# A gated mix of memory attention and a GLU: narrower memory update, new planner lengths and a seeded order of the fillers

## The chip, the core and the metric

The kernel runs on one core of a Trainium2 chip. The metric is the device time of one execution in microseconds; lower is better. An unprofiled run gives only that time. One more execution is recorded by the hardware profiler, and the profile and trace that are shown here come from it.

The engines are called as the profile calls them: PE is TensorE (its weight loads are PEld), DVE is VectorE, ACT is ScalarE, POOL is GpSimd, SP the engine that issues most of the DMAs.

## What is computed

`x` is 2048 x 512, bf16. Two branches work on it and a gate mixes them:

```python
g = sigmoid((x * gate_w).sum(-1))
out = g * attention(x) + (1 - g) * glu(x)

# glu: 512 -> 1792 -> 512
h = gelu(x @ w_gate) * (x @ w_up);  b = h @ w_down

# attention: 32 heads of 16, four segments of 512 rows, one after the other
for s in range(4):
    p = softmax(qs @ ks.T * 0.25 + causal_mask)
    a_dot = p @ vs
    a_mem = (phi(qs) @ M) / (phi(qs) @ z + 1e-6)     # phi(t) = t+1 if t > 0 else exp(t)
    o = sigmoid(beta) * a_mem + (1 - sigmoid(beta)) * a_dot
    M += phi(ks).T @ vs;  z += phi(ks).sum(rows)     # per head: 16 x 16 and 16
a = o @ wo
```

For each head M is a 16 x 16 block and z a vector of 16. Stored for eight heads on 128 partitions, M is a block-diagonal matrix.

## The kernel before

**Opening.** Weights and x are loaded over the SP queue, with transposing DMAs for the segments 1 to 3 of x. Then the gate half of the GLU runs for all segments at once: 28 `gate_pair` groups, each of eight 128x128 matmuls with 512 columns (L457), one gelu on ACT (L625) for each pair. Among them lies one tiny matmul, `f_bps` (L644), which spreads beta over the partitions; ACT takes its tanh (L673), and DVE derives `omg`, `ebr`, `bdeb` (block-diagonal mask times a factor) and the scaled `wo` from it. In the kernel before, this group stands after the seventh gate pair.

**Main part.** Each segment has 20 logit slots (`logit_slot`, L713). A slot's matmuls use row tiles: 16 or 32 rows, four heads at once. Each slot fills four PSUM banks (two pairs), ACT takes two exps of 128 x 1024 (L735), POOL zeroes what the causal mask hides (L744). Five slots give one chunk of eight heads; `pv_group` (L763) multiplies by v, DVE transposes the result, takes the reciprocal of its sum column and scales (L781 to L807). `N` (L799) and `r` times gate (L794) are operations with both inputs in SBUF.

Between two slots TensorE does fillers, the dense work: `up_group` (the other half of the GLU), `qk_group` and `v_group` for the next segment, `m_update`, `mem_den`, `mem_num`, and `out_group` (w_down and wo for the segment before). Dense products are split into four column tiles of 32 (L461), so that four matmuls run side by side. Each output of a filler is taken from PSUM by DVE or ACT.

**Memory.** `phi` makes an exp on ACT (L825), a maximum and a minimum on DVE (L829, L832), and an addition on POOL (L836). phi(k) is transposed by a DMA into `pk`. `m_update` multiplies it by v, with 8 heads x 17 columns (v and a one) at once: for each of two chunks and four row blocks, four column tiles of 32 weights by 136 columns, of which each tile needs only those of its own two heads. DVE adds the result to `Macc` (L882, L884); after the second pair, one operation makes `Mbd` (L891) and one `zbd` (L894), both with the diagonal masked.

**Order.** A planner in the kernel's file (`Sched`) sets the order of every engine's instructions before they are emitted. Each `add` gives a task its engine, an assumed length in ns, its dependencies, its PSUM banks and its priority. The planner runs a list schedule over these: on each engine the ready task with the lowest priority value goes first; logit slots have a due time, which spreads the remaining dense work over the remaining slots; rings of buffers and the eight PSUM banks hold tasks back. `NUPS` says how many up groups belong to each segment. The order is fixed in the program; each engine then runs its list in that order and waits where an input is late.

Of the kernel before, what the change touches and what calls it, by code (L numbers as in the profile page):

```python
# [1 line left out]

# [9 lines left out]
F32 = dt.float32  # L12

P = 128
D = 512
H = 32
DH = 16
VW = DH + 1
NSEG = 4
L = 512  # L20
KT = L // P
DFF = 1792
FC = D // P
NCH = H // 8
HS = DFF // P
# [9 lines left out]
NWARM = 7  # L35
NUPS = (28, 10, 9, 9)
SHAPES = {"gen": [(b,) for b in range(NBANK)],
# [16 lines left out]
class Sched:  # L54
# [7 lines left out]
    def __init__(self, rings):  # L62
        self.tasks = []
        self.bufs = rings

    def add(self, engs, cost, fn, **kw):

        engs = {engs: cost} if isinstance(engs, str) else dict(zip(engs, cost))
        t = Task(engs, fn, **kw)
        t.seq = len(self.tasks)  # L70
        self.tasks.append(t)
        return t
# [199 lines left out]
def kernel(  # L272
# [38 lines left out]
    def ctile(name, shape, dtype=BF):  # L311
        return cp.tile(shape, dtype, name=name, tag=name)
# [37 lines left out]
    Mbd = ctile("Mbd", [P, NCH, 8, DH])  # L350
    Macc = ctile("Macc", [P, NCH, 8, VW], F32)
    G2 = ctile("G2", [P, NSEG, QB], F32)
# [39 lines left out]
    def ext(at):  # L392
# [26 lines left out]
                            compare_op=ALU.is_ge, fill=0.0, base=DH - 1, channel_multiplier=-1)  # L419
    nc.gpsimd.memset(vz[1][:, :, :], 1.0)  # L420

    def group(name, cost, mms, prio, deps, alloc="gen", also=None, **kw):
# [11 lines left out]

    EV = {"DVE": 610, "ACT": 560}

# [31 lines left out]
    def odd_copy(s, c, ev):  # L468
        pr = c // 2
        ko = ("o", s, pr)  # L470

        def fo(e):
            if ko not in QK:
                QK[ko] = rtile("kO", [P, 2, L])
            nc.vector.tensor_scalar_mul(QK[ko][:, c % 2, :], QK[("k", s, pr)][:, c % 2, :],
                                        odd[:, :])
        new = ko not in first_ev
        o = add("DVE", 400, fo, prio=2, deps=[ev] + ([] if new else [first_ev[ko]]),
                alloc=["kO"] if new else [])
        first_ev.setdefault(ko, o)  # L480
        EVQK[("o", s, c)] = o
# [136 lines left out]
    def gate_pair(s, hp, prio):  # L618
        def mms(t):
            for i in range(2):  # L620
                mm_x(t[:, i, :], wga, (2 * hp + i) * P, s)
        g, box = group("gt", 8 * MM, mms, prio, [a_x[s], a_wg0 if hp < 2 else a_wga], alloc="pair")
        read_x[s].append(g)
        dst = G[:, s, 2 * hp:2 * hp + 2, :]
        ge = evac("ACT", g, box, lambda e, t: nc.scalar.activation(dst, t[:, :, :],  # L625
                                                                  AF.Gelu_apprx_tanh),
                  cost=960, ring="pair")
        GM[(s, hp)] = ge
        TAB["last_gt"], TAB["last_ge"] = g, ge
# [36 lines left out]
    for s in range(NSEG):  # L666
        if s == 3:
            gate_rows(-960 + 20 * s)
        for hp in range(HS // 2):
            gate_pair(s, hp, -959 + 20 * s + hp)  # L670
            if s == 0 and hp == HS // 2 - 1:
                g, box = group("bps", 60, f_bps, -942, [a_be])
                t_tb = evac("ACT", g, box, lambda e, t: nc.scalar.activation(  # L673
                    tb[:, :], t[:, 0:NCH], AF.Tanh, scale=0.5), cost=250)
                t_om = add("DVE", 100, f_omg, deps=[t_tb], prio=5)
                t_eb = add("DVE", 1200, f_eb, deps=[t_om], prio=5)
                t_wo = add("DVE", 1300, f_wo, deps=[t_om, a_wo], prio=7)
# [16 lines left out]
    def logit_slot(s, t):  # L694
# [37 lines left out]
        for h in range(2):  # L732
# [16 lines left out]
            XT_[(gi, h)] = x  # L749
            AT[(gi, h)] = add("POOL", 380 if w in (0, 3) else 610, fa, prio=0, deps=[x])  # L750

    def pv_group(s, c, e):
# [27 lines left out]
        def f_T(_, t):  # L780
            nc.vector.transpose(TT[key][:, e, :, :].rearrange("p a b -> p (a b)"), t[:, :])  # L781
        ev = evac("DVE", g, box, f_T)
        if e == 0:
# [22 lines left out]
        def f_o(_):  # L806
            nc.vector.transpose(xT[:, c, s * L:(s + 1) * L],  # L807
                                NN[key][:, :, :, :].rearrange("p a e d -> p (a e d)"))
        r = add("DVE", 280, f_r, prio=3, deps=[ev, NMT[("Te", key)]], alloc=["r"])
        rg = add("DVE", 120, f_rg, prio=3, deps=[r, TAB["g2"]])  # L810
        n = add("DVE", 650, f_n, prio=3, deps=[rg], alloc=["N"], frees=[("r", r), ("T", T0)])
        last = n
        if s > 0:
            last = add("DVE", 500, f_m, prio=3, deps=[n, NMT[("Nm", key)]],
                       frees=[("Nm", NMT[("Nm", key)])])
        OTT[key] = add("DVE", 640, f_o, prio=3, deps=[last] + read_x[s], frees=[("N", n)])

    PQ, PKt, PHI, PKD, RMt = {}, {}, {}, {}, {}

    def phi(src, deps, prio, mk, ring):  # L820
        box = {}

        def f_e(_):
            box["E"] = rtile("E", [P, 2, L])
            nc.scalar.activation(box["E"][:, :, :], src()[:, :, :], AF.Exp)  # L825

        def f_q(_):
            box["Q"] = rtile("Q1", [P, 2, L])
            nc.vector.tensor_scalar_max(box["Q"][:, :, :], src()[:, :, :], 0.0)  # L829

        def f_m(_):
            nc.vector.tensor_scalar_min(box["E"][:, :, :], box["E"][:, :, :], 1.0)  # L832

        def f_a(_):
            d = mk()
            nc.gpsimd.tensor_add(d[:, :, :], box["E"][:, :, :], box["Q"][:, :, :])  # L836
        e = add("ACT", 980, f_e, prio=prio, deps=deps + [TAB["first_x"], opened], alloc=["E"])
        q = add("DVE", 380, f_q, prio=5, deps=[e], alloc=["Q1"])
        m = add("DVE", 380, f_m, prio=5, deps=[e])
        return add("POOL", 2250, f_a, prio=5, deps=[m, q], alloc=[ring],  # L840
                   frees=[("E", e), ("Q1", q)])
# [23 lines left out]

    def m_update(s, pr, prio):
        def mms(t):
            for i in range(2):
                c = 2 * pr + i
                for kt in range(KT):  # L870
                    dense(t[:, i * 8 * VW:(i + 1) * 8 * VW], PKt[(s, pr)][:, i, kt, :],
                          vz[s % 2][:, kt, 8 * c * VW:8 * (c + 1) * VW], kt == 0, kt == KT - 1)
        g, box = group("M", 8 * 60, mms, prio,
                       [PKD[(s, pr)]] + [EVV[(s, kt)] for kt in range(KT)]
# [4 lines left out]
        def f_acc(e, t):  # L879
            dst = Macc[:, 2 * pr:2 * pr + 2, :, :].rearrange("p c h w -> p (c h w)")  # L880
            if s == 0:
                nc.vector.tensor_copy(dst, t[:, 0:16 * VW])  # L882
            else:
                nc.vector.tensor_add(dst, t[:, 0:16 * VW], dst)  # L884
        acc = evac("DVE", g, box, f_acc, cost=360)
        TAB[("acc", s, pr)] = acc
# [3 lines left out]
        def f_mbd(_):  # L890
            nc.vector.tensor_mul(Mbd[:, :, :, :], Macc[:, :, :, 0:DH], bdeb[:, :, :, :])  # L891

        def f_zbd(_):
            nc.vector.tensor_mul(  # L894
                zbd[:, :].rearrange("p (c n) -> p c n", c=NCH)[:, :, 0:P]
                .rearrange("p c (j m) -> p c j m", j=4)[:, :, :, 0:2],
                Macc[:, :, :, DH].rearrange("p c (j e) -> p c j e", j=4),
                bd[:, :, 0].rearrange("p (j e) -> p j e", j=4)[:, None, :, :]
                .to_broadcast((P, NCH, 4, 2)))
        deps = [TAB[("acc", s, 0)], acc, t_eb] + [TAB[("num", s, c)] for c in range(NCH) if s]  # L900
        TAB[("mbd", s)] = add("DVE", 620, f_mbd, prio=3, deps=deps)
        TAB[("zbd", s)] = add("DVE", 150, f_zbd, prio=3, deps=deps + ([TAB[("den", s)]] if s else []))

    def mem_den(s, prio):
# [25 lines left out]
        ev = evac("DVE", g, box, f_T)  # L930
        a = add("DVE", 200, f_a, prio=2, deps=[ev], alloc=["rm"], frees=[("Tm", g)])
        r = add("DVE", 880, f_r, prio=2, deps=[a])
        TAB[("rm", s)] = add("DVE", 250, f_g, prio=2, deps=[r])
        TAB[("rma", s)] = a

    def mem_num(s, c, prio):
# [13 lines left out]
        def f_n(_):  # L950
# [4 lines left out]
        ev = evac("DVE", g, box, f_T)  # L955
        NMT[("Nm", (s, c))] = add("DVE", 680, f_n, prio=2.5, deps=[ev, TAB[("rm", s)]],
                                  alloc=["Nm"], frees=[("Tm", g), ("rm", TAB[("rma", s)])])
# [15 lines left out]
    def out_group(s, qt, prio):  # L973
# [5 lines left out]
        for lo in range(0, HS, 2):  # L979
            def fn(_, lo=lo):  # L980
                down(bank(first), s, qt, lo, lo + 2, False)
            prev = add("PE", 2 * MM, fn, prio=prio, mode="more" if lo else "open",
                       deps=[prev] if lo else [UPT[(s, hs)] for hs in range(HS)] + [TAB["wdn"]]
                       + ([] if late else att), alloc=[] if lo else ["gen"], final=late)
            first = first or prev
# [4 lines left out]
        def fo(e):  # L990
# [4 lines left out]
            else:  # L995
                nc.vector.tensor_scalar_mul(bx["o"][:, :], bank(first), f)  # L996
        ev = add(["DVE", "ACT"], [670, 590], fo, deps=[g, TAB["omz"]], alloc=["osb"],
                 frees=[("gen", first)])
# [80 lines left out]
```

## Time and profile before

| | before |
|---|---|
| median of 3 runs | 282.32 us (282.3 to 283.6) |
| profiled execution, own time | 284.42 us |
| its span, first to last instruction | 282.7 us |
| busy: PE / DVE / ACT / POOL | 272.1 / 173.2 / 211.3 / 129.1 us |
| opening (0 to 67.1 us), PE busy | 64.6 us |
| logit slots (67.1 to 268 us), PE busy | 196.7 us |
| end (268 to 282.7 us), PE busy | 10.7 us |
| mean granted TensorE clock | 0.994 |

How to read it: a matmul's record is longer than the time until the next one starts, because matmuls are pipelined, so busy PE is not PE at its peak, and a hole between starts is larger than the idle time shown. Lines of the kernel are given as L and a number; L457 and L461 are in the helper `dense`, so most matmuls have one of these two, and the names of tiles tell them apart. In timelines a row has start, length, engine, line, what it writes and reads, shape, count, and in brackets the engine's idle time before it and what ended it. The row of the clock gives tenths of the full TensorE clock in forty slices of the span.

### The profile page before, as it was taken

Reading aid. Unit: us, or ns where it says so; the run is one execution under the profiler, and the core shown is the slowest. Engines: PE = TensorE matmul, PEld = TensorE weight load, DVE = VectorE, ACT = ScalarE, POOL = GpSimd, SP = SyncE. Lnnn points to the kernel's source line nnn. Section 1 sums busy time; section 2 is a strip of 40 time slices with the busy share of each in tenths; the row PEclk is TensorE's granted clock in tenths of the full one; section 3 lists DMA queues with packets and bytes.
Section 4 is the critical chain, followed back from the end, with each engine's and each line's share of the span. In section 5 each row is a group of like instructions: output and inputs, shape, how many; then the busy total and the mean of one; then the engine's idle time right before and its main releaser. Section 6 shows DMA issues by size and latency. Waiting matters only on the chain.

```text
span 282.7 us, 10149 instructions
## 1 busy us (share of the span) xinstructions
PE 272.1 (96%) x4498; PEld 126.6 (45%) x4504; DVE 173.2 (61%) x316; ACT 211.3 (75%) x231; POOL 129.1 (46%) x220
## 2 busy tenths in 40 slices
PE   8999899999999989999999999999999998999994
PEld 3444344444445444454445445444444443444541
DVE  2330210102879898989897797999758699535330
ACT  3545466457897777999898898898889889798520
POOL 8000000060565376486857477457645756444400
PEclk9999999999999999999999999999999998999999
DMA  7963970000022010020010020000000000000011
GB/s 237 345 125 77 339 252 2 0 0 2 3 42 39 2 39 2 2 42 2 21 39 22 3 58 23 3 2 2 21 21 22 2 21 3 21 21 21 23 38 39
DMA packets 22036, 14.02 MB, mean 50 GB/s; under 512 B 14056, under 2 KB 20968, under 8 KB 21992
## 3 DMA queue, kind: packets, MB, share of 16 engines
q1 hardware_dynamic: 21448, 12.85, 16.0%
q8 instruction: 35, 0.57, 0.9%
q10 hardware_dynamic: 544, 0.52, 0.6%
q14 instruction: 9, 0.07, 0.1%
HBM read 8.13 MB, written 2.10 MB: 36 GB/s over the span
## 4 chain that ended last, share of the span: by engine, by line
PE 74%; DVE 8%; SPq 7%; ACT 4%; DMA 2%; issue 2%; POOL 0%; ACTq 0%; DVEq 0%
PE ps L461 48%; PE ps L457 13%; PE ps L713 8%; SPq L360 7%; PE ps L763 5%; ACT pT L735 3%; DMA wdn<-in_A_x_dram 1%; DVE N L799 1%; DVE G L635 1%; DVE vz_82 L299 1%; DMA beta_76<-in_A_beta_dram 1%; DVE r L794 1%; DVE T L781 1%; DVE Nm L952 1%; DVE N L804 1%
## 5 line engine op out<-in xcount | busy, mean ns | idle before, releaser
L735 ACT ACTIVATE pT<-ps 128x1024 bf16<-128x1024 f32 x160 | 153.9, 1025 | 20.9 <-PE ps L713 20.2
L744 POOL TENSOR_SCALAR_AFFINE_SELECT pT<-pT 128x512 bf16<-128x512 bf16 (+1 forms) x160 | 92.5, 586 | 83.1 <-ACT pT L735 82.6
L461 PE MATMUL ps<-wdn,G 128*32 128x512 bf16 x896 | 59.3, 386 | 0.5 <-ACT pT L735 0.5
L461 PE MATMUL ps<-xT,wup 128*32 128x512 bf16 x896 | 55.2, 380 | 0.9 <-DVE G L635 0.8
L635 DVE TENSOR_TENSOR G<-ps,G 128x512 bf16<-128x512 f32 x56 | 37.6, 678 | 20.7 <-PE ps L461 20.3
L457 PE MATMUL ps<-xT,wga 128*128 128x512 bf16 x219 | 48.4, 379 | 0.4 <-issue 0.2
L625 ACT ACTIVATE G<-ps 128x1024 bf16<-128x1024 f32 x28 | 28.7, 1025 | 24.2 <-PE ps L457 23.5
L457 PEld LDWEIGHTS <-wga 128*128 128x128 bf16 x224 | 21.8, 98 | 26.4 <-issue 0.4
L461 PEld LDWEIGHTS <-wup 128*32 128x32 bf16 x896 | 22.3, 96 | 22.9 <-issue 4.7
L461 PEld LDWEIGHTS <-G 128*32 128x32 bf16 x896 | 21.9, 97 | 21.3 <-issue 3.9
L781 DVE STREAM_TRANSPOSE T<-ps 128x512 f32<-128x512 f32 x32 | 22.7, 708 | 13.6 <-PE ps L763 13.4
L596 POOL COPY G_87<-tt 32x16 f32<-32x16 f32 x16 | 3.1, 195 | 49.3 <-DVE tt L588 48.6
L713 PE MATMUL ps<-qT,kT 16*128 16x256 bf16 (+2 forms) x320 | 17.9, 273 | 1.5 <-DVE vz_82 L299 1.2
L713 PE MATMUL ps<-qT,kO 32*128 32x128 bf16 (+2 forms) x320 | 18.5, 276 | 0.1
L461 PEld LDWEIGHTS <-xT 128*32 128x32 bf16 x448 | 11.4, 96 | 11.3 <-issue 1.6
L461 PE MATMUL ps<-wo,xT 128*32 128x512 bf16 x256 | 16.5, 379 | 0.0
L713 PEld LDWEIGHTS <-kT 16*128 16x128 bf16 x320 | 6.9, 92 | 19.4 <-issue 19.1
L799 DVE TENSOR_TENSOR N<-T,r 128x512 bf16<-128x512 f32 x16 | 14.2, 887 | 0.4
L713 PEld LDWEIGHTS <-kO 32*128 32x128 bf16 x320 | 7.1, 93 | 14.8 <-issue 14.6
L994 ACT ACTIVATE osb<-ps,omz 128x512 bf16<-128x512 f32 x6 | 4.1, 687 | 11.5 <-PE ps L461 11.5
L996 DVE TENSOR_SCALAR osb<-ps,omz 128x512 bf16<-128x512 f32 x10 | 7.4, 743 | 8.6 <-PE ps L461 8.5
L461 PE MATMUL ps<-xT,wk 128*32 128x512 bf16 x192 | 12.5, 380 | 0.0
(116 smaller groups left out, 282.1 us busy)
## 6 DMA issues: line engine op xcount, KB each, us to landing
out_dram<-osb SPq DMA_DIRECT2D x16, 128.0 KB, 1.7
wup<-in_B_w_up_dram SPq DMA_DIRECT2D x1, 1792.0 KB, 8.1
wdn<-in_B_w_down_dram SPq DMA_DIRECT2D x1, 1792.0 KB, 13.5
wga<-in_B_w_gate_dram SPq DMA_DIRECT2D x1, 1280.0 KB, 10.3
wq<-in_A_wq_dram SPq DMA_DIRECT2D x1, 512.0 KB, 6.0
wga<-in_B_w_gate_dram SPq DMA_DIRECT2D x1, 512.0 KB
wv<-in_A_wv_dram SPq DMA_DIRECT2D x1, 512.0 KB, 7.9
wo<-in_A_wo_dram SPq DMA_DIRECT2D x1, 512.0 KB, 9.1
```

The costliest lines, as they stand in the source:

```text
L360: nc.sync.dma_start_transpose(xT[:, fc, s * L:(s + 1) * L], x2[s * L:(s + 1) * L, fc * P:(fc + 1) * P])
L457: nc.tensor.matmul(t, lhsT=lhsT, rhs=rhs, start=start, stop=stop)
L461: nc.tensor.matmul(t[a, :], lhsT=lhsT[:, a], rhs=rhs, start=start, stop=stop, tile_position=(0, 32 * j), skip_group_check=True)
L625: ge = evac("ACT", g, box, lambda e, t: nc.scalar.activation(dst, t[:, :, :], AF.Gelu_apprx_tanh), cost=960, ring="pair")
L635: UPT[(s, hs)] = evac("DVE", g, box, lambda e, t: nc.vector.tensor_mul(G[:, s, hs, :], t[:, :], G[:, s, hs, :]))
L713: nc.tensor.matmul(A[j // 2][:, j % 2, at * P:(at + nq) * P], lhsT=l, rhs=r, start=True, stop=True, tile_position=(32 * j, 0))
L735: nc.scalar.activation(pT[(s, t, h)][:, :, :], A[h][:, :, :], AF.Exp, scale=0.25)
L744: nc.gpsimd.affine_select(out=v, in_=v, pattern=pat, compare_op=ALU.is_ge, fill=0.0, base=0, channel_multiplier=-1)
L763: nc.tensor.matmul(t[32 * j:32 * j + 32, qb * P:(qb + nq) * P], lhsT=vz[s % 2][:, kt, h * VW:h * VW + 32], rhs=pT[(s, t0 + w, j // 2)][:, ...
L781: nc.vector.transpose(TT[key][:, e, :, :].rearrange("p a b -> p (a b)"), t[:, :])
L799: nc.vector.tensor_mul(NN[key][:, :, :, :].rearrange("p a e d -> p e a d"), TT[key][:, :, :, 0:DH], RR[key][:, :, :, :].to_broadcast((P, 2 ...
L996: nc.vector.tensor_scalar_mul(bx["o"][:, :], bank(first), f)
```

## The change

- `m_update` gives each of the four column tiles only the v columns of its own two heads: 34 columns instead of 136. `Macc` shrinks from 8 x 17 to 2 x 17 per chunk. `Mbd` is cleared once by POOL in the opening, and is then written only on the diagonal, by four operations of 32 partitions. `zbd` reads the smaller `Macc` with a broadcast.
- The planner's assumed lengths of some twenty operations are replaced by others; the due times and priorities follow from them.
- The priorities of TensorE's fillers get a random addition of up to 2.0 either way, from a seeded generator.
- `NUPS` goes from (28, 10, 9, 9) to (26, 12, 10, 8).
- beta's small matmul stands after the last gate pair of segment 1 instead of segment 0.
- `out_group` waits for `att[:ATT]` with ATT = 5; `att` has five entries.

```diff
-NUPS = (28, 10, 9, 9)
+NUPS = (26, 12, 10, 8)
+ATT = 5
+SEED = 18
+SPREAD = 2.0
...
     def add(self, engs, cost, fn, **kw):
 
+        if "PE" in engs and 0 < kw["prio"] < 9000:
+            kw["prio"] += self.rng.uniform(-SPREAD, SPREAD)
...
-    Macc = ctile("Macc", [P, NCH, 8, VW], F32)
+    Macc = ctile("Macc", [P, NCH, 2, VW], F32)
...
     nc.gpsimd.memset(vz[1][:, :, :], 1.0)
+    nc.gpsimd.memset(Mbd[:, :, :, :], 0.0)
...
-    EV = {"DVE": 610, "ACT": 560}
+    EV = {"DVE": 605, "ACT": 495}
...
-            if s == 0 and hp == HS // 2 - 1:
-                g, box = group("bps", 60, f_bps, -942, [a_be])
+            if s == 1 and hp == HS // 2 - 1:
+                g, box = group("bps", 60, f_bps, -922, [a_be])
...
-        r = add("DVE", 280, f_r, prio=3, deps=[ev, NMT[("Te", key)]], alloc=["r"])
-        rg = add("DVE", 120, f_rg, prio=3, deps=[r, TAB["g2"]])
-        n = add("DVE", 650, f_n, prio=3, deps=[rg], alloc=["N"], frees=[("r", r), ("T", T0)])
+        r = add("DVE", 260, f_r, prio=3, deps=[ev, NMT[("Te", key)]], alloc=["r"])
+        rg = add("DVE", 245, f_rg, prio=3, deps=[r, TAB["g2"]])
+        n = add("DVE", 800, f_n, prio=3, deps=[rg], alloc=["N"], frees=[("r", r), ("T", T0)])
...
             for i in range(2):
-                c = 2 * pr + i
                 for kt in range(KT):
-                    dense(t[:, i * 8 * VW:(i + 1) * 8 * VW], PKt[(s, pr)][:, i, kt, :],
-                          vz[s % 2][:, kt, 8 * c * VW:8 * (c + 1) * VW], kt == 0, kt == KT - 1)
-        g, box = group("M", 8 * 60, mms, prio,
+                    for j in range(4):
+                        a = slice(32 * j, 32 * j + 32)
+                        h = 16 * pr + 8 * i + 2 * j
+                        nc.tensor.matmul(t[a, 2 * i * VW:2 * (i + 1) * VW],
+                                         lhsT=PKt[(s, pr)][:, i, kt, a],
+                                         rhs=vz[s % 2][:, kt, h * VW:(h + 2) * VW],
+                                         start=(kt == 0), stop=(kt == KT - 1),
+                                         tile_position=(0, 32 * j), skip_group_check=True)
+        g, box = group("M", 8 * 28, mms, prio,
...
-        acc = evac("DVE", g, box, f_acc, cost=360)
+        acc = evac("DVE", g, box, f_acc, cost=200)
...
         def f_mbd(_):
-            nc.vector.tensor_mul(Mbd[:, :, :, :], Macc[:, :, :, 0:DH], bdeb[:, :, :, :])
+            for j in range(4):
+                a, hh = slice(32 * j, 32 * j + 32), slice(2 * j, 2 * j + 2)
+                nc.vector.tensor_mul(Mbd[a, :, hh, :], Macc[a, :, :, 0:DH], bdeb[a, :, hh, :])
...
-                Macc[:, :, :, DH].rearrange("p c (j e) -> p c j e", j=4),
+                Macc[:, :, :, DH][:, :, None, :].to_broadcast((P, NCH, 4, 2)),
...
-        TAB[("mbd", s)] = add("DVE", 620, f_mbd, prio=3, deps=deps)
-        TAB[("zbd", s)] = add("DVE", 150, f_zbd, prio=3, deps=deps + ([TAB[("den", s)]] if s else []))
+        TAB[("mbd", s)] = add("DVE", 560, f_mbd, prio=3, deps=deps)
+        TAB[("zbd", s)] = add("DVE", 335, f_zbd, prio=3, deps=deps + ([TAB[("den", s)]] if s else []))
...
-                       + ([] if late else att), alloc=[] if lo else ["gen"], final=late)
+                       + ([] if late else att[:ATT]), alloc=[] if lo else ["gen"], final=late)
```

Other assumed lengths in the change, old to new in ns: odd copy 400 to 320; gelu 960 to 920; mask 380/610 to 400/635; the transpose after PV 610 to 625; adding the memory part 500 to 490; the transpose into x 640 to 610; phi's exp 980 to 960, maximum and minimum 380 to 330 and 345, addition 2250 to 2090; den's three operations 200/880/250 to 120/860/285; num's product 680 to 765; the output's eviction 670/590 to 660/585. The length of the logit exps stays at 920.

More of the change, by code (lines that the diff above doesn't have):

```diff
@@ L1 @@
 from contextlib import ExitStack
+from random import Random
 import concourse.bass as bass
@@ L64, in __init__ @@
         self.bufs = rings
+        self.rng = Random(SEED)
     def add(self, engs, cost, fn, **kw):
+        if "PE" in engs and 0 < kw["prio"] < 9000:
+            kw["prio"] += self.rng.uniform(-SPREAD, SPREAD)
         engs = {engs: cost} if isinstance(engs, str) else dict(zip(engs, cost))
@@ L477, in odd_copy @@
         new = ko not in first_ev
-        o = add("DVE", 400, fo, prio=2, deps=[ev] + ([] if new else [first_ev[ko]]),
+        o = add("DVE", 320, fo, prio=2, deps=[ev] + ([] if new else [first_ev[ko]]),
                 alloc=["kO"] if new else [])
@@ L626, in gate_pair @@
                                                                   AF.Gelu_apprx_tanh),
-                  cost=960, ring="pair")
+                  cost=920, ring="pair")
         GM[(s, hp)] = ge
@@ L749, in logit_slot @@
             XT_[(gi, h)] = x
-            AT[(gi, h)] = add("POOL", 380 if w in (0, 3) else 610, fa, prio=0, deps=[x])
+            AT[(gi, h)] = add("POOL", 400 if w in (0, 3) else 635, fa, prio=0, deps=[x])
     def pv_group(s, c, e):
@@ L781, in f_T @@
             nc.vector.transpose(TT[key][:, e, :, :].rearrange("p a b -> p (a b)"), t[:, :])
-        ev = evac("DVE", g, box, f_T)
+        ev = evac("DVE", g, box, f_T, cost=625)
         if e == 0:
@@ L808, in f_o @@
                                 NN[key][:, :, :, :].rearrange("p a e d -> p (a e d)"))
-        r = add("DVE", 280, f_r, prio=3, deps=[ev, NMT[("Te", key)]], alloc=["r"])
-        rg = add("DVE", 120, f_rg, prio=3, deps=[r, TAB["g2"]])
-        n = add("DVE", 650, f_n, prio=3, deps=[rg], alloc=["N"], frees=[("r", r), ("T", T0)])
+        r = add("DVE", 260, f_r, prio=3, deps=[ev, NMT[("Te", key)]], alloc=["r"])
+        rg = add("DVE", 245, f_rg, prio=3, deps=[r, TAB["g2"]])
+        n = add("DVE", 800, f_n, prio=3, deps=[rg], alloc=["N"], frees=[("r", r), ("T", T0)])
         last = n
         if s > 0:
-            last = add("DVE", 500, f_m, prio=3, deps=[n, NMT[("Nm", key)]],
+            last = add("DVE", 490, f_m, prio=3, deps=[n, NMT[("Nm", key)]],
                        frees=[("Nm", NMT[("Nm", key)])])
-        OTT[key] = add("DVE", 640, f_o, prio=3, deps=[last] + read_x[s], frees=[("N", n)])
+        OTT[key] = add("DVE", 610, f_o, prio=3, deps=[last] + read_x[s], frees=[("N", n)])
     PQ, PKt, PHI, PKD, RMt = {}, {}, {}, {}, {}
@@ L836, in f_a @@
             nc.gpsimd.tensor_add(d[:, :, :], box["E"][:, :, :], box["Q"][:, :, :])
[L837 to L840, printed above, removed]
+        e = add("ACT", 960, f_e, prio=prio, deps=deps + [TAB["first_x"], opened], alloc=["E"])
+        q = add("DVE", 330, f_q, prio=5, deps=[e], alloc=["Q1"])
+        m = add("DVE", 345, f_m, prio=5, deps=[e])
+        return add("POOL", 2090, f_a, prio=5, deps=[m, q], alloc=[ring],
                    frees=[("E", e), ("Q1", q)])
@@ L879, in f_acc @@
         def f_acc(e, t):
-            dst = Macc[:, 2 * pr:2 * pr + 2, :, :].rearrange("p c h w -> p (c h w)")
+            dst = Macc[:, 2 * pr:2 * pr + 2, :, :].rearrange("p c e w -> p (c e w)")
             if s == 0:
-                nc.vector.tensor_copy(dst, t[:, 0:16 * VW])
+                nc.vector.tensor_copy(dst, t[:, 0:4 * VW])
             else:
-                nc.vector.tensor_add(dst, t[:, 0:16 * VW], dst)
-        acc = evac("DVE", g, box, f_acc, cost=360)
+                nc.vector.tensor_add(dst, t[:, 0:4 * VW], dst)
+        acc = evac("DVE", g, box, f_acc, cost=200)
         TAB[("acc", s, pr)] = acc
@@ L930, in mem_den @@
         ev = evac("DVE", g, box, f_T)
-        a = add("DVE", 200, f_a, prio=2, deps=[ev], alloc=["rm"], frees=[("Tm", g)])
-        r = add("DVE", 880, f_r, prio=2, deps=[a])
-        TAB[("rm", s)] = add("DVE", 250, f_g, prio=2, deps=[r])
+        a = add("DVE", 120, f_a, prio=2, deps=[ev], alloc=["rm"], frees=[("Tm", g)])
+        r = add("DVE", 860, f_r, prio=2, deps=[a])
+        TAB[("rm", s)] = add("DVE", 285, f_g, prio=2, deps=[r])
         TAB[("rma", s)] = a
@@ L955, in mem_num @@
         ev = evac("DVE", g, box, f_T)
-        NMT[("Nm", (s, c))] = add("DVE", 680, f_n, prio=2.5, deps=[ev, TAB[("rm", s)]],
+        NMT[("Nm", (s, c))] = add("DVE", 765, f_n, prio=2.5, deps=[ev, TAB[("rm", s)]],
                                   alloc=["Nm"], frees=[("Tm", g), ("rm", TAB[("rma", s)])])
@@ L996, in fo @@
                 nc.vector.tensor_scalar_mul(bx["o"][:, :], bank(first), f)
-        ev = add(["DVE", "ACT"], [670, 590], fo, deps=[g, TAB["omz"]], alloc=["osb"],
+        ev = add(["DVE", "ACT"], [660, 585], fo, deps=[g, TAB["omz"]], alloc=["osb"],
                  frees=[("gen", first)])
```

## The prediction

> **What bounds the kernel now.** I read the page first, then the busy time by stretch, then TensorE's timeline wherever a stretch had a hole.
>
> ```profile
> span 282.7 us, 10149 instructions
> PE 272.1 (96%) x4498; PEld 126.6 (45%) x4504; DVE 173.2 (61%) x316; ACT 211.3 (75%) x231; POOL 129.1 (46%) x220
> PEclk9999999999999999999999999999999998999999
> ```
>
> TensorE is busy for 96% of the span, so time comes only from less TensorE work, from holes in it, or from the one slice with a lower clock. In stretches (length, then busy time of PE, PEld, DVE, ACT, POOL, then granted clock):
>
> ```profile
> 93.90:104.00 10.10, 8.91 (x200) 4.38 (x200) 9.13 (x15) 7.84 (x10) 5.88 (x7) 1.00 0.07 15
> 160.00:190.00 30.00, 28.58 (x592) 13.61 (x588) 27.38 (x48) 26.67 (x30) 17.86 (x26) 1.00 0.08 20
> 232.20:238.10 5.90, 4.80 (x84) 2.05 (x84) 5.87 (x12) 5.54 (x7) 3.53 (x7) 1.00 0.02 4
> 238.30:241.70 3.40, 3.40 (x45) 1.29 (x40) 3.03 (x5) 2.23 (x4) 2.11 (x3) 0.50 0.00 0
> ```
>
> The holes lie where VectorE is over 90% busy, and 3.4 us ran at half clock. TensorE's timeline there, and at two other places (start, length, instructions, wait):
>
> ```profile
> 29.55 0.16 PE L644 MATMUL ps<-beta_76,hot_78 8*128 8x4 bf16 x1 [0.68 <-DMA beta_76<-in_A_beta_dram]
> ...
> 85.16 0.66 PE L461 MATMUL ps<-vz_81,pk 128*32 128x136 bf16 x32
> ...
> 103.42 0.27 PE L713 MATMUL ps<-qT,kT 16*128 16x256 bf16 x1 [1.19 <-DVE vz_82 L299]
> ...
> 235.64 0.28 PE L713 MATMUL ps<-qT,kT 16*128 16x256 bf16 x2 [0.33 <-ACT pT L735]
> 235.65 1.30 PE L713 MATMUL ps<-qT,kO 32*128 32x256 bf16 x8
> 237.47 0.61 PE L461 MATMUL ps<-wdn,G 128*32 128x512 bf16 x8 [0.53 <-ACT pT L735]
> ```
>
> A matmul's record is longer than its turn (0.38 us against 0.21), so a hole is larger than the idle shown. I measure it from start to start, less the usual step. The holes after the warm-up are then: beta 0.84 (28.50 to 29.55); 1.36 at 101.95; 0.46 at 139.9; 0.81 and 0.24 at 166.8 and 169.6; four of 0.2 to 0.4 (88.5, 180.5, 184.1, 189.0), 1.3 together; and 2.1 between 233.8 and 238.1, where work of 2.3 us took 4.36. The half clock adds 1.7. Why the hole at 102 is there:
>
> ```profile
> 100.09 2.13 POOL L836 TENSOR_TENSOR pkT<-E,Q_1317 128x1024 bf16<-128x1024 bf16 x1
> 100.20 2.57 DVE L799 TENSOR_TENSOR N<-T,r 128x512 bf16<-128x512 f32 x1
> ```
>
> N usually takes 0.69 (the median of 16). Begun under GpSimd's addition it lasted until that was over, and the v eviction behind it, which the next logit slot waited for, was late. The holes at 139.9 (Nm, 1.53 us instead of 0.85) and at 166.8 (r times gate, 1.36 instead of 0.2) have the same neighbour. So 2.9 of the 4.2 us in the middle of the kernel are VectorE blocked under GpSimd's addition.
>
> **The change part by part.**
>
> *Memory update on TensorE.* Six groups of 32 matmuls go from 136 columns to 34. Before, a group takes 85.16 to 85.64, 0.48 us: 60 ns for each set of four column tiles, 15 ns per matmul. No row has a tiled matmul under 128 columns, so I bound it: by columns alone 15 ns per set (a group 0.12); 60 if nothing is gained. The Trainium skill, TensorE: Matmul & The Clock Gate, section "Wait — 56ns, not 53.3ns?", says that starts are never closer than about 25 ns however few the columns, and TensorEngine Tiling (Array Packing), "Instruction Overhead", advises against tiling a dimension that is already small. Read per instruction, that is 100 ns per set, 0.80 us per group: 6 x 0.32 = 1.9 us lost. But the row above already has a start every 15 ns, so a floor of that kind can only hold within one tile; then a set costs 25 to 28 ns. I take 27: 0.22 us per group, a gain of 6 x 0.26 = **1.6 us**, with ends of -2.2 and +1.9.
>
> *Memory update on VectorE.* Evictions L882/L884 (387 and 439 ns at 272 elements) fall to 68 elements; the 128-wide L922 took 205 ns, so about 200 to 250: 1.1 us less over six. Mbd goes from one operation of 910 ns to four on 32 partitions and 128 elements. Nearest rows: 252 ns (L655) and 368 ns (L928), so 1.0 to 1.5 us instead of 0.9. A rule speaks against this: SBUF — State Buffer, "SBUF: two separate sides", says that a VectorE operation with two SBUF inputs and a GpSimd operation that reads SBUF exclude each other for a whole instruction. By it each of the four can wait for a mask of 0.45 to 0.68 us: up to 3.6 us per update; by the rows 1.1. The one of before already took 694 to 1119 ns with that neighbour, so I take 1.3 each, 1.2 us more over three. zbd stays at 0.42. Together nothing on VectorE. The cover is that M is needed only by the next segment's den and num; without it, 2 us at three places. The new memset of Mbd stands last of GpSimd's opening; L420 (2240 wide) took 1.96 us, so 0.45, ending near 7.7 us. GpSimd's next work comes at 54 us, so it costs nothing.
>
> *beta's matmul* moves behind seven more gate pairs (1.7 us each, to about 41 us). beta landed at 29.4; the SP queue is unchanged. **0.84 us** gained. tanh goes later on ScalarE, which idles 24 us among the gelus; omg, bdeb and the scaling of wo (which waited 5.0 us for its DMA) have until the first output group.
>
> *Planner lengths, seed, NUPS* alter only the order; TensorE's total work stays. ATT = 5 keeps all five entries of att, so nothing changes there. I counted the instructions that stand between successive logit slots (80, from 0), at the rows' steps: dense group of 16 matmuls 0.87 us, PV 0.55, num 0.22, a slot itself with its two changes of tiling 0.42. Each slot brings ScalarE two exps, 1.93 us.
> - Before, slots 65 to 67 hold a num and an up; a PV; nothing: 2.9 us of TensorE against 5.8 of exps. That is the hole at 234. In the new order they hold 2.15, 2.15 and 1.83, and no slot is under 1.5. So **2.1 us** of hole go, and with them, I judge, the half clock that began as the hole ended: **1.7**. The filler comes from behind the last slot: TensorE work there falls from 15.2 to 13.5.
> - New short stretches: slots 20 to 24 (TensorE 11.6, ScalarE 13.1, VectorE 14.1) and 40 to 44 (9.2, 10.3, 12.1). ScalarE is short by 1.5 and 1.1; TensorE can wait less, as exps lag by part of a slot, or all of it, not below 0. I take half: 1.3.
> - Port collisions: in the new order an operation with two SBUF inputs follows the minimum, within the 2.1 us of the addition, in five of twelve cases (N in the 5th and 6th, Mbd in the 7th, r times gate in the 8th, rm times gate in the 10th), against three before. By what is left of the addition when they come, VectorE loses 1.2 + 1.2 + 3 x 0.5 = 3.9 us, as against 3.7 before (1.9 + 0.7 + 1.2). So TensorE loses about 3.0 again (range 0 to 4). Other small waits 0.6.
> - Middle waits: 1.3 + 3.0 + 0.6 = 4.9 against 4.2, **0.7 lost**.
> - Evictions: osb goes four times from VectorE (0.74) to ScalarE (0.69). The last four are all on ScalarE, one each 0.87 us of matmuls or more, so it keeps up; the last is on ScalarE in both. No change at the end.
>
> **Sum.** Span 282.7 - 0.84 - 1.6 - 2.1 - 1.7 + 0.7 = 277.2. The profiled execution took 284.42, 1.7 more than its span, and would take 278.9. The median of the runs is 282.32; the same 5.5 us less gives **276.8**.
>
> **Rivals.**
> - Waits get rarer: half of the old 4.2 instead of 4.9, so 274.0. For: remeasured lengths of VectorE operations (N 800, zbd 335). Against: exp stays planned at 920 where it takes 965, and five collisions are in the order.
> - A hole at the start of segment 1 (slots 20 to 31): the whole 2.6 of exp shortfall shows and a half clock follows it: +1.3 + 1.7, so 279.8. For: 14.1 us of VectorE in 11.6. Against: at slots 40 to 49 before, VectorE had 27.0 in 22.0 and TensorE lost 1.0.
> - The narrow matmuls keep a floor per instruction, so the change doesn't do what it says: +3.5, so 280.3. Against: 15 ns per start in the row.
> - Slower: VectorE's queue at slots 20 to 31. Work above TensorE's, carried on from slot to slot, reaches 7.8 us at slot 30. If all of it reaches TensorE instead of some 2.2, that is +5.6, and two windows of half clock +3.4: 285.8. It decides from 5.5 us of extra loss there. Against: banks and rings let VectorE lag; 7.0 by the same count at slot 47 before cost 1.0.
>
> **How the numbers follow.** Chances: forecast 0.58 (own range 274.5 to 279), rarer waits 0.14, hole in segment 1 0.18, floor 0.05, slower 0.05. What a measurement can tell from no change is 0.5%, 1.4 us: 280.9 to 283.7. Under it lie the first two, most of the third and half of the fourth: 0.91; within 0.05; above 0.04. Range 273.0 to 281.0: down past the rarer waits by the unknown end of the narrow matmuls, up over the hole and the floor; the slower case is left out.
>
> **What would show it.** Right: no wait for beta; 128x34 groups of about 0.22 us; no stretch near slot 66 and no clock under 1.0 in it; N of 1.5 us or more under GpSimd's additions in segment 0's end and segment 1. Wrong: a group of 0.5 us or more; PE idle above 3 us between 115 and 150; another half-clock window.

## The result: 279.3 us instead of 283.0

The median is 279.32 us (four executions, 279.01 to 279.73), against 282.96 for the kernel before in the same sessions. The ratio is 0.987, with a 95% interval from 0.983 to 0.991. The forecast was 276.8, so 3.6 us came off where 5.5 were forecast.

The profiled executions show a larger step, 282.7 to 277.7 us of span, and the forecast for that was 277.2. So the sum was nearly right against the profile and too large against the median. Why is the subject of two of the points below.

The page of the changed kernel, and the same kind of stretches as before:

```profile
span 277.7 us, 10149 instructions
PE 268.0 (96%) x4498; PEld 125.4 (45%) x4504; DVE 172.0 (62%) x322; ACT 212.6 (77%) x234; POOL 130.0 (47%) x221
PEclk9999999999999999999999999999999999999999
```

```profile
93.00:103.00 10.00, 10.00 (x224) 4.62 (x220) 9.32 (x20) 8.44 (x10) 6.67 (x9) 1.00 0.01 3
126.00:142.00 16.00, 13.43 (x287) 6.60 (x290) 15.31 (x28) 13.89 (x17) 11.50 (x14) 1.00 0.11 19
160.00:190.00 30.00, 29.02 (x644) 14.00 (x638) 26.09 (x49) 27.28 (x31) 19.61 (x30) 1.00 0.09 22
230.50:239.00 8.50, 8.50 (x172) 3.72 (x168) 5.50 (x11) 7.63 (x9) 6.33 (x9) 1.00 0.02 8
```

The stretch around 234 us has no hole and no half clock any more. The holes now gather between 126 and 142 us. TensorE's timeline of the changed kernel there and at one narrow memory update:

```profile
84.31 0.38 PE L882 MATMUL ps<-vz_81,pk 128*32 128x34 bf16 x32
84.53 1.05 PE L469 MATMUL ps<-xT,wup 128*32 128x512 bf16 x15
...
132.34 0.40 PE L469 MATMUL ps<-pq,Mbd 128*32 128x512 bf16 x4 [0.88 <-DVE G L643]
...
133.56 1.05 PE L469 MATMUL ps<-xT,wup 128*32 128x512 bf16 x16 [0.38 <-DVE T L789]
...
141.55 0.83 PE L469 MATMUL ps<-wv,xT 128*32 128x512 bf16 x11 [1.28 <-DVE vz_81 L306]
```

A narrow group takes 84.31 to 84.53, 0.22 us instead of 0.48. The waits in the list come to 5.0 us by starts, counting holes over 0.15 us, against 4.2 before without the hole at 234. Their causes stand on VectorE and GpSimd (both engines, the changed kernel):

```profile
126.99 2.13 POOL L844 TENSOR_TENSOR pkT<-E,Q_1949 128x1024 bf16<-128x1024 bf16 x1
127.61 2.04 DVE L807 TENSOR_TENSOR N<-T,r 128x512 bf16<-128x512 f32 x1
...
138.54 2.09 POOL L752 TENSOR_SCALAR_AFFINE_SELECT pT<-pT 128x256 bf16<-128x256 bf16 x4
138.76 2.01 DVE L907 TENSOR_TENSOR Mbd<-Macc,bdeb 32x128 bf16<-32x128 f32 x4
140.80 0.69 DVE L306 CAST vz_81<-ps 128x512 bf16<-128x512 f32 x1
```

The first pair is the old collision at a new place: N is held until GpSimd's addition is over and ends about 0.55 us after it (alone it takes 0.69). The second is new: the four small products for Mbd alternate with four masks and take 2.0 us together, and the eviction of v that TensorE waits for (the last row) stands behind them.

### The profile page after: what moved, and what is told of

It reads as the page before. It is cut to its first block, busy times and chain, and to the rows that moved or that the text cites. A ratio compares the mean times of both kernels' runs of the same rounds, so it can differ in the third digit from the quotient of the medians.

```text
span 277.7 us, 10149 instructions
## 1 busy us (share of the span) xinstructions
PE 268.0 (96%) x4498; PEld 125.4 (45%) x4504; DVE 172.0 (62%) x322; ACT 212.6 (77%) x234; POOL 130.0 (47%) x221
## 4 chain that ended last, share of the span: by engine, by line
PE 85%; DVE 11%; DMA 1%; issue 1%; ACT 1%; DVEq 0%; ACTq 0%
PE ps L469 49%; PE ps L465 20%; PE ps L721 8%; PE ps L771 5%; DMA wdn<-in_A_x_dram 1%; DVE Tm L964 1%; PE ps L552 1%; DVE T L789 1%; DVE G L643 1%; DVE Mbd L907 1%; DVE Nm L968 1%; DVE N L807 1%; PE ps L538 1%; DVE rm L941 1%; DVE Tm L934 1%
## 5 line engine op out<-in xcount | busy, mean ns | idle before, releaser
L469 PE MATMUL ps<-xT,wup 128*32 128x512 bf16 x896 | 55.9, 380 | 1.1 <-DVE Tm L964 0.4
L721 PE MATMUL ps<-qT,kT 16*128 16x256 bf16 (+2 forms) x320 | 17.3, 274 | 0.0
L721 PE MATMUL ps<-qT,kO 32*128 32x128 bf16 (+2 forms) x320 | 17.2, 272 | 0.0
L1010 ACT ACTIVATE osb<-ps,omz 128x512 bf16<-128x512 f32 x10 | 6.9, 688 | 10.6 <-PE ps L469 9.4
L469 PE MATMUL ps<-wv,xT 128*32 128x512 bf16 x192 | 12.2, 380 | 1.3 <-DVE vz_81 L306 1.3
L807 DVE TENSOR_TENSOR N<-T,r 128x512 bf16<-128x512 f32 x16 | 13.1, 818 | 0.4
L306 DVE CAST kT<-ps 128x512 bf16<-128x512 f32 x11 | 7.5, 691 | 8.4 <-PE ps L469 5.8
```

The lines of the kernel that those rows point to most:

```text
L306: nc.vector.tensor_copy(dst, src)
L469: nc.tensor.matmul(t[a, :], lhsT=lhsT[:, a], rhs=rhs, start=start, stop=stop, tile_position=(0, 32 * j), skip_group_check=True)
L721: nc.tensor.matmul(A[j // 2][:, j % 2, at * P:(at + nq) * P], lhsT=l, rhs=r, start=True, stop=True, tile_position=(32 * j, 0))
L807: nc.vector.tensor_mul(NN[key][:, :, :, :].rearrange("p a e d -> p e a d"), TT[key][:, :, :, 0:DH], RR[key][:, :, :, :].to_broadcast((P, 2 ...
L1010: nc.scalar.activation(bx["o"][:, :], bank(first), AF.Copy, scale=f)
```

## The experiments

The median of the kernel before depends on how many of its executions hold a window of half clock: 19 of the 44 executions in the session of the first four experiments had a mean clock of 0.994 or less, and took 283.74 us (median), the other 25 took 282.41. So I compare with the 282.41 of full-clock executions where a difference under 2 us matters. The changed kernel's 279.32 comes from the session of the result alone; between the later sessions the full-clock median of the kernel before moved by 0.2 us (282.41 and 282.60), so differences of that size from 279.32 say nothing.

**The narrow memory update alone, in the order of before.** `m_update`, `Macc`, `Mbd` and `zbd` are those of the change; all planner lengths are those of before, and every engine's list has the same order.

```diff
-                    dense(t[:, i * 8 * VW:(i + 1) * 8 * VW], PKt[(s, pr)][:, i, kt, :],
-                          vz[s % 2][:, kt, 8 * c * VW:8 * (c + 1) * VW], kt == 0, kt == KT - 1)
+                    for j in range(4):
+                        a = slice(32 * j, 32 * j + 32)
+                        h = 16 * pr + 8 * i + 2 * j
+                        nc.tensor.matmul(t[a, 2 * i * VW:2 * (i + 1) * VW],
+                                         lhsT=PKt[(s, pr)][:, i, kt, a],
+                                         rhs=vz[s % 2][:, kt, h * VW:(h + 2) * VW],
...
-            nc.vector.tensor_mul(Mbd[:, :, :, :], Macc[:, :, :, 0:DH], bdeb[:, :, :, :])
+            for j in range(4):
+                a, hh = slice(32 * j, 32 * j + 32), slice(2 * j, 2 * j + 2)
+                nc.vector.tensor_mul(Mbd[a, :, hh, :], Macc[a, :, :, 0:DH], bdeb[a, :, hh, :])
```

> The kernel before with the narrow memory update alone; every engine's order is that of before. Theory (the sum of the prediction, with the 0.23 us per group that the changed kernel's trace shows): six groups at 0.23 instead of 0.48 us, so about 1.5 us less than the kernel before in the same session, less what runs into waits that are there anyway: 0.5 to 1.5 us less. Rival (the narrow matmuls pay per instruction, or the four masked products on VectorE cost as much): no change or up to 2 us more. Second question: if the profiled span still holds a window at half clock, the mean clock is 0.994 and the execution is about 1.7 us longer than those whose mean clock is 1.0; the theory is that this window comes and goes between executions of the order of before.

Measured: 282.50 us against 282.79, ratio 0.9995 (0.9976 to 1.0014); with full clock 282.27 against 282.41. No gain that can be measured. The starts of the logit slots in the two traces show why. Counted from the start of slot 0, five of the six updates bring the next slot forward by 0.23 to 0.27 us, as expected, and one by 0.13. But slot 12 gives 0.22 back, slot 13 gives 0.31 back, and slots 48 and 49 give 0.63 back; at the end 0.22 is left of 1.3. At slot 12 VectorE is blocked under an addition until the same moment as before, so TensorE only waits longer. The cause at slot 13 isn't shown. At slots 48 and 49 the split of Mbd is the cause (VectorE in this run, then TensorE):

```profile
191.76 2.29 DVE L899 TENSOR_TENSOR Mbd<-Macc,bdeb 32x128 bf16<-32x128 f32 x4
194.09 0.69 DVE L636 TENSOR_TENSOR G<-ps,G 128x512 bf16<-128x512 f32 x1
```

```profile
194.83 0.38 PE L714 MATMUL ps<-qT,kO 32*128 32x256 bf16 x9 [0.35 <-DVE G L636]
```

Four products take 2.29 us where the single one of before took 0.69 to 1.12; the G behind them ends at 194.8, and the rest of slot 48 and slot 49, which wait for it, start there. In the kernel before TensorE had no wait at this place.

**The wide update put back, in the order of the changed kernel.** `Macc`, its evictions, `zbd` and the opening's memset go back with it.

```diff
-                    for j in range(4):
-                        a = slice(32 * j, 32 * j + 32)
-                        h = 16 * pr + 8 * i + 2 * j
-                        nc.tensor.matmul(t[a, 2 * i * VW:2 * (i + 1) * VW],
...
+                    dense(t[:, i * 8 * VW:(i + 1) * 8 * VW], PKt[(s, pr)][:, i, kt, :],
+                          vz[s % 2][:, kt, 8 * c * VW:8 * (c + 1) * VW], kt == 0, kt == KT - 1)
...
-            for j in range(4):
-                a, hh = slice(32 * j, 32 * j + 32), slice(2 * j, 2 * j + 2)
-                nc.vector.tensor_mul(Mbd[a, :, hh, :], Macc[a, :, :, 0:DH], bdeb[a, :, hh, :])
+            nc.vector.tensor_mul(Mbd[:, :, :, :], Macc[:, :, :, 0:DH], bdeb[:, :, :, :])
```

> The changed kernel with the wide memory update put back; every engine's order is that of the changed kernel. Theory: 6 x 0.25 = 1.5 us more than the changed kernel (279.3), so about 280.8, if TensorE's work is what counts; less than 0.5 us more if the narrow update's time went into waits. Rival (the split masked products cost more than the narrow matmuls save): faster than the changed kernel.

Measured: 279.14 us, against 279.32 for the changed kernel. So the narrow update brings nothing in this order either. The slots show the same exchange from the other side: five of the six wide groups cost 0.16 to 0.25 us at the next slot, and the hole at 140 us, 1.27 us of it, is gone, since there is no split Mbd in front of that v eviction. It is not a clean exchange: another N now begins 0.20 us after an addition, not 0.02 us before one, takes 2.48 us instead of 0.68, and slot 18 loses 0.93 us behind it, while 0.2 to 0.4 us come back at some other slots. So that the two updates end within 0.2 us of each other is in part chance. What is left of the change in time is the order's (and beta's).

**beta's matmul alone.**

```diff
-            if s == 0 and hp == HS // 2 - 1:
+            if s == 1 and hp == HS // 2 - 1:
```

> The kernel before with beta's small matmul after the second segment's gate pairs; nothing else moves. Theory: the 0.84 us wait goes and the slots start 0.8 us earlier, 0.8 us less than before. Rival (the wait only moves, since something later is bound by a DMA or by ScalarE): no change.

Measured: 281.99 against 282.79, ratio 0.9971 (0.9957 to 0.9986), 0.8 us; among executions with full clock 281.92 against 282.41, 0.5.

**The changed kernel without the random addition.**

```diff
-SPREAD = 2.0
+SPREAD = 0.0
```

> The changed kernel without the random addition to the priorities (spread 0). Theory: the order is one among many of about the same quality, with waits of 4 to 8 us in the middle: 279 to 282. Rival (the seed was chosen, and most of the gain is in it): 282 or more.

Measured: 283.98 us, 1.0048 of before (1.0027 to 1.0069). Beta's move, the narrow update, the new lengths and the new NUPS together are slower than before; it is the seed's order that makes the change faster, by 4.7 us. This order has no empty slots (the least holds 1.7 us of TensorE work) and no half clock. But the gaps between the turns of its matmuls (a turn is 0.21 us for 512 columns, less for fewer in proportion), counted over 0.15 us among the slots, come to 11.0 us, against 6.4 in the changed kernel, and that is the difference. It also has 7.8 us of VectorE time blocked under additions, against 3.7: this is what the VectorE operations that run under a GpSimd addition take beyond their usual length.

**GpSimd's addition taken out, in three orders.** To see how much of that is the collisions, the addition in `phi` becomes a memset of the same tile (0.95 to 1.0 us, no input). phi is then 1 and the memory branch isn't computed; the order of every engine stays.

```diff
-            nc.gpsimd.tensor_add(d[:, :, :], box["E"][:, :, :], box["Q"][:, :, :])
+            nc.gpsimd.memset(d[:, :, :], 1.0)
```

> The kernel before with GpSimd's addition in phi replaced by a memset of the same tile: phi is then 1, so the memory branch isn't computed; every engine's order is that of before. Theory (VectorE's operations with two SBUF inputs are blocked under the addition, and TensorE waits for what stands behind them): the holes at 102, 139.9 and 166.8 us (2.9 us together) go or shrink under 0.3 each, and 1.5 to 2.9 us come off, some of it taken again by other waits. Rival (those holes have another cause): less than 0.7 us.

> The changed kernel without the random addition (measured 283.98), with the same memset in place of the addition in phi (the memory branch isn't computed). Its trace has 7.8 us of VectorE blocked under additions, the changed kernel's 3.7. Theory: this difference is most of the 4.7 us between the two orders, so here 3 to 5 us come off (279 to 281) and the two orders come within 2.5 us of each other. Rival (the order without the seed is slower for how TensorE's and ScalarE's work lies in the slots): under 1.5 us comes off, the difference stays above 3.5.

> The changed kernel with the same memset in place of the addition in phi (the memory branch isn't computed). Theory: the holes at 131 and 132.8 us (1.5 us) go and 1 to 2.5 us come off 279.3. Rival: under 0.5 us.

| order | with the addition | with the memset | off |
|---|---|---|---|
| before, full clock | 282.41 | 279.5 and 279.9 | 2.7 |
| without the random addition | 283.98 | 279.06 | 4.9 |
| seed 18 | 279.32 | 277.73 | 1.6 |

The same N as at 100 us before, now beside the memset (both engines, the kernel before with the memset):

```profile
99.77 0.94 POOL L836 MEMSET pkT<- 128x1024 bf16 x1
99.90 0.69 DVE L799 TENSOR_TENSOR N<-T,r 128x512 bf16<-128x512 f32 x1
```

N runs while the memset runs, and takes its usual 0.69 us instead of 2.57. So it is not that GpSimd is busy which holds N, but this addition. In the order of before, the holes at 102, 139.9 and 166.8 us are gone or under 0.2 us, and those at 181, 186 and 232 (times of this run), which had other causes, stand as before (gaps of 0.5, 0.4, and 0.5 with 0.7 us, in both). The difference between the two orders of the changed kernel shrinks from 4.7 to 1.3 us. So up to 3.3 us of the seed's 4.7 are collisions that it happens to avoid. The memset also takes half of the addition's time off GpSimd and ends a wait for the minimum, and some of the 3.3 may be theirs; the next experiment leaves both in.

**The addition cut in pieces.** The same sum in four instructions of 256 columns, first in the order of the changed kernel and then in the one without the random addition; and in two of 512 columns.

```diff
-            nc.gpsimd.tensor_add(d[:, :, :], box["E"][:, :, :], box["Q"][:, :, :])
+            for i in range(2):
+                for h in range(2):
+                    c = slice(256 * h, 256 * h + 256)
+                    nc.gpsimd.tensor_add(d[:, i, c], box["E"][:, i, c], box["Q"][:, i, c])
```

> The changed kernel with GpSimd's addition in phi cut into four of 256 columns; same result, same order. Theory (the lock on the shared access is held for one instruction): a blocked operation waits for one piece of about 0.6 us instead of up to 2.1, so N under the addition takes at most 1.4 us instead of 2.0, and 0.5 to 1.5 us come off 279.3. Rival (both engines merely share the access, or the next piece takes it again before VectorE gets it): N as long as before, no gain, and up to 0.5 us more for the longer additions.

Measured: 278.33 us, 1.0 off. The same N as above, in this run (both engines):

```profile
126.83 3.51 POOL L847 TENSOR_TENSOR pkT<-E,Q 128x256 bf16<-128x256 bf16 x4
127.46 0.64 DVE L807 TENSOR_TENSOR N<-T,r 128x512 bf16<-128x512 f32 x1
...
128.63 1.18 DVE L971 TENSOR_TENSOR Nm<-Tm,rm 128x512 bf16<-128x512 f32 x1
```

N takes 0.64 us between two pieces, where it took 2.04; now GpSimd waits instead (one piece takes 1.18 us), and its four pieces need 3.51 us. A piece alone takes 0.67 us, so the four are 0.6 longer than the one of 2.13.

> The changed kernel without the random addition, with phi's addition on GpSimd cut into four of 256 columns. In the changed kernel's order the cut took 1.0 us off, of 1.6 that the memset took. Theory: the same share here, about 60% of 4.9, so 2.5 to 3.5 us off 283.98: 280.5 to 281.5. Rival (the longer additions make masks late, and that is dearer in an order that is full): under 1.5 us off.

Measured: 281.45 us, 2.5 off 283.98, so about half of what the memset took. With the cut alone the two orders come 1.5 us closer (2.5 off against 1.0). So of the seed's 4.7 us the collisions are between about 1.5 and 3.3; for the rest no run here has the cause.

```diff
-            nc.gpsimd.tensor_add(d[:, :, :], box["E"][:, :, :], box["Q"][:, :, :])
+            for i in range(2):
+                nc.gpsimd.tensor_add(d[:, i, :], box["E"][:, i, :], box["Q"][:, i, :])
```

> The changed kernel with phi's addition on GpSimd cut into two of 512 columns. Four pieces took 2.7 us in all instead of 2.1 and made masks late (TensorE waited 0.7 and 0.5 us for them at 130 us). Theory: two pieces cost about 2.3 us in all, keep most of the shorter block, and come to 277.8 to 278.6, at or under the 278.33 of four pieces. Rival: N comes under a piece of 1.1 us and loses half of the gain: 278.8 or more.

Measured: 278.00 us (277.65 to 278.59), 0.9821 of before (0.9782 to 0.9859). Two pieces of 1.20 us each (the mean) are as good as four; the difference of 0.3 us between them is within the spread of four executions each. This is the best whole kernel of the study, 1.3 us under the changed one.

**Other seeds.**

```diff
-SEED = 18
+SEED = 3
```

> The changed kernel with seed 3 instead of 18. Its order again has almost no TensorE work in slots 65 to 67 (1.2, 0.4 and 0.6 us by count). Theory: a hole of 1.5 us or more there, and a window at half clock in part of the executions (mean clock 0.995 or less); 281 to 284. Rival (the half clock of before came from something else): no execution under 0.997.

Measured: 283.63 us, 1.0013 of before (0.9990 to 1.0035). Of 20 executions 6 had full clock (282.24 us), 9 a mean clock of 0.992 to 0.994 (283.64), and 5 one of 0.987 or 0.988 (284.86): this fits none, one and two windows of 3.4 us at half clock, each worth 1.2 to 1.4 us (one window is what the profiled execution shows). The profiled one, by its stretches and on TensorE:

```profile
228.00:234.00 6.00, 5.24 (x115) 2.50 (x107) 5.90 (x12) 5.22 (x7) 2.64 (x7) 1.00 0.01 3
234.00:240.00 6.00, 5.01 (x60) 1.96 (x61) 5.93 (x12) 5.60 (x7) 4.63 (x7) 0.78 0.00 1
```

```profile
234.79 0.40 PE L469 MATMUL ps<-pq,Mbd 128*32 128x512 bf16 x4 [0.30 <-ACT pT L743]
235.71 0.75 PE L721 MATMUL ps<-qT,kO 32*128 32x512 bf16 x4 [0.52 <-ACT pT L743]
```

Before the clock falls, TensorE has work for hardly half of the time, in pieces, with no more than 0.91 us between two starts. In this order slots 65 to 67 hold 1.2, 0.6 and 0.4 us of TensorE work. In the orders of seed 18, of seed 2 and without the random addition no slot holds under 1.5, and none of their executions, with whole or cut additions, fell under a mean clock of 0.997 (44 executions).

```diff
-SEED = 18
+SEED = 2
```

> The changed kernel with seed 2. No slot has less than 1.5 us of TensorE work. Theory: no execution under a mean clock of 0.997; the time goes with the VectorE time that is lost under additions, read from its trace (280 at 4 us of it, 283 at 8). Rival: a half-clock window in spite of the full slots, or a time that does not follow the collisions.

Measured: 282.47 us, 0.9989 of before (0.9970 to 1.0008), with a mean clock of 0.997 or more in all 12 executions. Its trace has 5.8 us under additions, for which the expectation's line gives 281.3: missed by 1.2. So the time under additions orders these kernels only roughly. The wide update in the order of seed 18 has 5.3 us of it and takes 279.14. My reading is that what counts is whether the blocked operation has something behind it that TensorE needs soon: in seed 2 a transposed output of PV and an eviction of q were behind (holes of 1.4 and 1.2 us). The blocked operations there were not of the kind with two SBUF inputs: `rm`<-`Tm` (1.78 us instead of 0.22) and an odd copy of k (2.22 instead of 0.35) each read one tensor and a factor.

## Why the prediction was right in sign and too large

1. *beta, 0.84 us:* right. The slots start at 66.30 instead of 67.09 us, and alone it brought 0.8 (0.5 with full clock). One pair of traces is a weak proof, since the opening itself varies: over all traces the slots start at 66.2 us in the mean without beta's wait (eleven traces, 65.65 to 66.92) and at 66.8 with it (three).
2. *Narrow update on TensorE, 6 x 0.26 = 1.6 us:* the price of a group was right (0.22 us; no floor per instruction holds across the four column tiles: 32 starts in 0.22 us are 7 ns each, 28 ns for a set of four, against the 25 ns per start that the prediction quotes). What failed is "a gain of": the gain does not reach the end, 0.2 us in one order and none in the other. TensorE was priced as the bound at these places, and the next wait was set by VectorE.
3. *Narrow update on VectorE, nothing together:* the sizes were near (Macc 0.19 to 0.23 us; Mbd 1.5, 2.0 and 1.5 where 1.3 was taken). "The cover is that M is needed only by the next segment's den and num" failed: what is late is not M but the next eviction in VectorE's queue, G or v, and that costs TensorE 0.6 to 1.3 us at one place of each order. The rule of SBUF — State Buffer, which I weighed and discounted, describes what the rows show (product and mask take turns), but its most, 3.6 us per update, was not reached: 2.0 here, 2.3 in the order of before.
4. *The hole at slots 65 to 67, 2.1 us:* right for this order: TensorE is busy for all of the 8.5 us there. Seed 3 has such a hole again, but its order differs elsewhere too, so no run prices the hole alone.
5. *Half clock, 1.7 us:* right in the profiled execution, but wrong for the median. "The same 5.5 us less" assumed that the profiled execution stands for all. Its 284.42 lay 2.1 above the median, and that was the sign: it was one of the 43% of executions with the window, which costs 1.3 us, so in the mean 0.6. With that share the forecast would have been 277.9, without the term 278.5. Full clock against full clock, 3.1 us came off (282.41 to 279.32), where the sum without this term gives 3.8.
6. *New waits, 0.7 us lost:* the sum of 4.9 met 5.0 by luck, for the places are others. 1.3 of the 5.0 is the hole at 140 us, which the split Mbd makes, so it is the narrow update's lost gain of point 2 seen from the other side. Of the five collisions named, two came (N in the sixth addition, rm times gate in the tenth); N in the fifth was in time, r times gate in the eighth was not held, and Mbd met masks, not an addition. The list named only operations with two SBUF inputs; the odd copy of k, with one, was held too (0.83 us instead of 0.35, at 108.7 us). ScalarE's shortfall at slots 20 to 24 and 40 to 44, 1.3 in the sum, was 0.3.
7. *The rivals:* no half clock in segment 1 and no loss of VectorE's whole lag, so neither the third case nor the slower one. Of what "planner lengths, seed, NUPS" do, the text looked only at the one order that was given. It did not say that the lengths and NUPS without the seed could be slower, and they are.

## What to carry to other kernels

When several engines are nearly full and run fixed lists, work taken from the busiest one shortens the time only where the next wait is its own; look at what it waits for next before counting the gain, by the starts of a marker such as the logit slots in both traces. Ask of the profiled execution where it lies among the runs: what only it shows (here a window of half clock) goes into the median with its share. And a planned order is one draw from a wide spread, 279 to 284 us for four orders of the changed kernel here; find what makes the bad draws bad, such as a long GpSimd instruction with VectorE work held under it, and shorten that.

## What the hardware showed that I had not expected

- A window of 3.4 us at half clock comes in some executions of the same program and not in others (19 of 44; 14 of 20 for seed 3), after a few us in which TensorE has work for about half of the time, without any gap of 1 us. The Trainium skill, TensorE: Matmul & The Clock Gate, Part 1, ties the lower clock to an idle window of that length, and says that the windows run freely. The first doesn't hold here, since no idle gap came near 3.4 us. The second fits the traces: in all four that hold such a window (before, narrow alone, beta alone, seed 3) the clock falls 232.106 us after its first rise to full (by the trace's record of the clock), which is 68.0 times the 3.413 us that it then stays down. It would let the same thin stretch fall into one window in one execution and into two in another; no run here tests that.
- Work for half of the time is not the whole condition. In the 3.4 us just before the clock fell, TensorE was busy (by its records) for 2.46 us in before and for 2.41 in seed 3. Without the random addition it was busy for only 2.04 of the 3.4 us from 173.5 us on (a whole step of that length, counted from the first rise), and the clock stayed full, there and in all seven executions. What it goes by stays open.
- VectorE's block under GpSimd lasts to the end of the instruction (in every trace an N held by an addition ends 0.55 us after it, about 0.14 less than N takes alone), and cutting that instruction lets VectorE in between the pieces: N went from 2.04 to 0.64 us.
- Four products on 32 partitions cost 1.4 to 2.3 us together in the changed kernel and in the narrow update alone, with masks beside them, and 0.24 each at best; the one on 128 partitions took 0.7 to 1.1. Whether one masked product with a broadcast, for the narrow `Macc`, keeps the gain of the narrow matmuls wasn't tried.
